# A list schedule with later K sets, a two-queue transfer model and second-stage sets not kept apart

## The chip, the cores and the metric

The kernel runs on one NeuronCore of a Trainium2 chip. The metric is the device time of one execution in microseconds (us). Five engines work side by side, each in its own instruction order: TensorE (PE; its weight loads are shown apart as PEld), VectorE (DVE), ScalarE (ACT), GpSimd (POOL) and SyncE (SP). Transfers between HBM and on-chip memory are issued from SP's, POOL's and ACT's queues. Matrix products land in PSUM banks, from which VectorE and ScalarE copy or combine them.

## The reference

Input `x` is 2048 tokens of 512 channels. A gate per token mixes two branches:

```python
g = sigmoid((x * gate_w).sum(-1, keepdims=True))
a = irfft(rfft(x^T, 2L) * rfft(K, 2L))[:L]^T + x * D_skip     # branch A, along the 2048 tokens
b = ((x @ w_gate) * (x @ w_up)) @ w_down                      # branch B, inner width 1792
out = g * a + (1 - g) * b
```

In branch A the convolution kernel is `K[d, l] = 2 Re(sum_n C[d,n] exp(A[d,n] dt[d] l))`, with 128 complex terms for each of the 512 channels; `A`, `C` and `dt` are computed from parameters.

## The kernel before

Branch B is most of the work. Each matmul operand in 32-bit precision is split in a high and a low part, and a product is three full-size matmuls (high x low, low x high, high x high), which the profile names by their tiles: `pg` and `pu` (gate and up products from tokens `xs` and weights `whi`, `wlo`), then `y` (down products from `hh`, `hl` and `dhi`, `dlo`). The 14 slices of the inner width are worked in four groups, and within a group the tokens in four blocks. VectorE multiplies `pu` by a copy of `pg` to `h`, ScalarE rounds `h` to `hh`, VectorE forms the rest `hl`. ScalarE scales finished `y` to `acc`, which is added to the output in HBM.

Branch A computes K and the transforms as small tiled matmuls between these. In 16 blocks of 32 channels, `phases`, `direct_powers`, `x_table` and `v_table` fill two tables, `x` and `v`, on VectorE and ScalarE; `k_block` multiplies them on TensorE, one K set of 128 matmuls into one bank (`k<-v,x`), and ScalarE and VectorE combine that to `kt`. After four blocks a quarter of the channels has its K. `k_first` transforms it (`k<-kt,w1k_t`, two sets) and stores it to `sk_d`; `u_part` has done the same with the input (`k<-in,w2s` in 64x512, eight sets early on) into `su_d`. `transforms` then runs, for each quarter, four second-stage sets (`m_second`, `k<-in,w2s` in 32x512; `x` or `v` in place of `in` in the last quarter), the products on VectorE (`m_product`), two inverse sets (`m_inverse`, `k<-y,w3s`) and the last stage (`m_last`, `k<-in,w4_t` or `k<-x,w4_t`, in the profile `w_t`). Data goes through HBM between the stages: POOL loads `su_d` and `sk_d`, SP stores and loads `y_d`.

All these small sets take their banks from one pool of four (`bank`, tag `k`). A K set takes one bank, the other sets take four at once, and a bank comes free when ScalarE or VectorE has read it.

The order of everything is a list schedule. Each piece of work is put down with `add(engine, us, fn, r=, w=, ...)`: its engine, a cost in the plan's time units and what it reads and writes. `Work.run` then repeatedly starts, of all pieces whose inputs are there, the one that can start first by the plan's own clock, with `rank` deciding between equals. Only the order that comes out of this is used: every engine issues its instructions in that order, and on the chip semaphores make them wait for one another. Three parts of the plan matter here:

- `inputs` and `ready`: a piece is ready when its inputs end in the plan, plus a small lag.
- `many`: a piece with `many > 0` starts no earlier than that many units behind the end of the last such piece on TensorE (`APART` = 6, `LESS` = 4 in the last two quarters). K sets, first-stage, second-stage and inverse sets of the K path have it.
- transfers: one bus in the plan, on which they run one after the other at `DMA_RATE`, with fixed lags.

All instructions are recorded through one helper, so nearly every row of the profile has its line, L124, and rows are told apart by their tiles.

Of the kernel before, what the change touches and what calls it, by code (L numbers as in the profile page):

```python
# [20 lines left out]
KT = D // P  # L21
# [94 lines left out]
class InOrder:  # L116


    def __init__(self, tc, engine):
        self.tc, self.engine, self.last = tc, engine, None  # L120
# [46 lines left out]
        self.deps, self.tiles, self.start, self.end, self.rows, self.many = set(), [], None, None, (), 0  # L167


class Work:  # L170


# [11 lines left out]


    APART, LESS = 6.0, 4.0
    DMA_RATE = 0.3

    def __init__(self):
        self.tags, self.tasks = {}, []  # L190
# [4 lines left out]
    def memory(self):  # L195
        return Tile(self, None, None, None, None, None, False)

    def add(self, engine, us, fn, r=(), w=(), rank=1, after=0.0, dma=0, hold=(), rows=(), many=0):


        task = Task(len(self.tasks), engine, us, fn, rank, after, dma)
        task.rows, task.many = rows, many
        self.tasks.append(task)
        clash = lambda p, q: p is None or q is None or p == q
        split = lambda x: x if isinstance(x, tuple) else (x, None)
        for tile, part in map(split, r):
            task.deps.update(t for p, t in tile.writers if clash(p, part))
        for tile, part in map(split, w):
            task.deps.update(t for p, t in tile.writers + tile.readers if clash(p, part))
        for tile, part in map(split, r):  # L210
            tile.readers.append((part, task))
        for tile, part in map(split, w):
            tile.writers.append((part, task))
        for tile, _ in map(split, [*r, *w, *hold]):
            if tile.pool and tile not in task.tiles:
                task.tiles.append(tile)
                tile.users.append(task)
        task.deps.discard(task)
        return task

    def ready(self, task, d):

        if d.engine == task.engine == "pe":
            return d.end
        return d.end + self.LAG.get(task.engine, 0.03) + (self.PE_LAG if d.engine == "pe" else 0.0)

    def inputs(self, task):

        at = task.after
        for d in task.deps:  # L230
            if d.end is None:
                return None
            at = max(at, self.ready(task, d))
        return at

    def slots(self, task, at):

# [30 lines left out]
    def run(self):  # L268
        left = {}
        for t in self.tasks:  # L270
            left.setdefault(t.engine, []).append(t)
        free = {e: 0.0 for e in left}
        bus, order, known, rows, apart = 0.0, [], {}, {}, -9.0
        while any(left.values()):
            best, wanted, found = None, {}, []
            for e, tasks in left.items():
                for t in tasks:
                    at = known.get(t)
                    if at is None:
                        at = self.inputs(t)  # L280
                        if at is None:
                            continue
                        known[t] = at
                    found.append((t, at))
                    if self.kept_waiting(t):
                        continue
                    for tile in t.tiles:
                        if tile.loose and tile.made is None:
                            wanted.setdefault(tile.key, []).append((t.rank, at))
            for t, ins in found:  # L290
                at = self.slots(t, ins)
                if at is None:
                    continue
                start = max([at, free[t.engine]] + [apart + t.many] * (t.many > 0) + [rows[r] for r in t.rows if r in rows])
                if any(
                    rank < t.rank and when <= start
                    for tile in t.tiles if tile.made is None and tile.loose for rank, when in wanted[tile.key]
                ):
                    continue
                key = (start, t.rank, t.n)  # L300
                if best is None or key < best[0]:
                    best = (key, t)
            assert best, "no work can start"
            (start, _, _), t = best
            left[t.engine].remove(t)
            if t.many:
                apart = start + t.us
            t.start, t.end = start, start + t.us
            free[t.engine] = t.end - self.OVERLAP.get(t.engine, 0.0)
            if t.dma:  # L310
                bus = max(bus, t.end + 1.3) + t.dma / self.DMA_RATE / 1000
                t.end = bus + 0.5
            rows.update((r, t.end) for r in t.rows)
            for tile in t.tiles:
                if tile.made is None:
                    tile.made = start
                    tile.had.append(tile)
            order.append(t)
        for t in order:
            t.fn()  # L320
        return order
# [3 lines left out]
def gated_mix_kernel(  # L325
# [19 lines left out]
    work = Work()  # L345
    add = work.add
# [247 lines left out]
    def evacuate(gi, ci, r, y):  # L594
        t = 4 * ci + r
        final = gi == len(GROUPS) - 1 and ci == LAST
        if final and r > 1:
            ending.append((r, y))
            return
        acc = new("glu", "acc", [P, D], bufs=3)  # L600
        add(
            "act", 0.69, lambda: act.activation(acc.t, y.t, AF.Copy, scale=ngate[:, t : t + 1]),
            r=[y, (m_gate, ci)], w=[acc], rank=0,
        )
        if final:
            ending.append((r, acc))
        elif gi == 0:
            add("sp", 0.42, lambda: sp.dma_start(ov[:, t, :], acc.t), r=[acc], w=[(m_out, t)], dma=256)
        else:
            add(  # L610
                "pool", 0.95, lambda: pool_q.dma_start(ov[:, t, :], acc.t, accum_op=ALU.add),
                r=[acc, (m_out, t)], dma=640, rows=[t],
            )

    def ends():
# [422 lines left out]
    def apart_of(q):  # L1038
        return work.LESS if q >= KT - 2 else work.APART

    def k_block(b, x, v):
        pk = bank()

        def kgen():
            pv = pk.t.rearrange("p (g j) -> p g j", j=64)
            for d in range(TB):
                ch, g = d % 4, d // 4
                for c in range(2):
                    pe.matmul(
                        pv[32 * ch : 32 * ch + 32, g, :], x.t[:, c, d, :], v.t[:, c, d, :], start=c == 0, stop=c == 1,  # L1050
                        tile_position=(0, 32 * ch),
                    )

        if b % 4 == 0:
            kts["now"] = new("tab", "kt", [P, 2, 2, 32, 16])
        kt, g0 = kts["now"], b % 4 * 8
        add("pe", 2.15, kgen, r=[x, v], w=[pk], rank=0, hold=[kt], many=work.APART)
        pv = lambda a: pk.t.rearrange("p (g a b k) -> p g a b k", a=2, b=2, k=16)[:, :, a]
        side = lambda h: kt.t[:, h, :, g0 : g0 + 8].rearrange("p b g k -> p g b k")
        add("act", 0.37, lambda: act.copy(side(1), pv(0)[:, :, :, ::-1]), r=[pk], w=[(kt, (1, b % 4))])  # L1060
        for h, op in enumerate((ALU.add, ALU.subtract)):
            add(
                "dve", 0.42, lambda h=h, op=op: dve.tensor_tensor(out=side(h), in0=pv(1), in1=side(1), op=op),
                r=[pk, (kt, (1, b % 4))], w=[(kt, (h, b % 4))], rank=0,
            )
        if b % 4 == 3:
            k_first(b // 4, kt)
# [89 lines left out]
    def m_second(q, T, ins, w):  # L1157
# [13 lines left out]
                to = banks[r].t[32 * c : 32 * c + 32].rearrange("l (p d) -> l p d", p=2)[:, p]  # L1171
                pe.matmul(to, w.t[lanes, m], src[lanes, c, p], start=True, stop=True, tile_position=(32 * r, 32 * c))

        add("pe", 1.05, fn, r=[*parts, w], w=banks, rank=1, hold=[to], many=apart_of(q))
        for r in range(4):
            h, e = divmod(r, 2)
            evict(
# [36 lines left out]
    def m_inverse(q, T0, ys, ws):  # L1214
# [18 lines left out]
                                    ys[t].t[lanes, k, e, cs], start=k == 0, stop=k == 1, tile_position=(32 * j, 64 * e),  # L1233
                                )

        add("pe", 2.13, fn, r=[*ys, *ws], w=[*banks, (m_turn, (q, T0))], rank=1, hold=sts, many=apart_of(q))
        for j in range(4):
            st, m = sts[j // 2], j % 2
            evict(
# [3 lines left out]
        for h in range(2):  # L1243
            st = sts[h]
            for p in range(2):
                b0 = 32 * (T0 + p) + 16 * h
                add(
                    "sp", 0.42,
                    lambda b0=b0, st=st, p=p: sp.dma_start(
                        y_d[q, b0 : b0 + 16].rearrange("(u e) n d -> (e n) u d", u=8),  # L1250
                        st.t[p::2].rearrange("p t i j d -> p (t i j) d"),
                    ),
                    r=[st], w=[(m_y, (q, T0 + h, p))], dma=256,
                )


# [7 lines left out]
    def m_last(q, gs):  # L1264
# [30 lines left out]
        for g, t, n0, n in pieces:  # L1295
# [30 lines left out]
            if n == 1 and n0 == LAST % 2:  # L1326
# [5 lines left out]
            add(  # L1332
                "pool", 0.95,
                lambda rs=rs, flat=flat: pool_q.dma_start(ov[:, rs[0] : rs[-1] + 1, cs], flat(), accum_op=ALU.add),
                r=[*parts, *((m_out, r) for r in rs)], dma=160 * len(rs), rows=rs,
            )

    def transforms(q):
# [111 lines left out]
```

## Time and profile before

| | |
|---|---|
| median of three runs | 591.4 us (590.39 to 591.89) |
| profiled execution | 592.45 us, of which the profile's span 590.6 us |
| TensorE busy | 576.8 us, 98% of the span |
| VectorE busy | 512.5 us, 87% |
| ScalarE busy | 400.0 us, 68% |
| GpSimd busy | 113.6 us, 19% |
| mean granted TensorE clock | 0.996 |

A row of a timeline reads: start, duration, engine, line, operation, the tiles written and read, shapes, count; in brackets the idle time ahead of it and what ended that. The granted clock (PEclk) is the share of full speed at which TensorE was allowed to run. Busy times of matmuls overlap, since they are pipelined: the cost of one in a row of equals is the step from start to start. The page's waits list who waited for whom: total, times, longest.

### The profile page before, as it was taken

How to read it: one execution, taken by the hardware profiler on the slowest of the kernel's cores; microseconds unless marked ns; L12 is line 12 of the kernel's file. 1: busy time of each engine (PE TensorE's matmuls, PEld its weight loads, DVE VectorE, ACT ScalarE, POOL GpSimd, SP SyncE). 2: the span in 40 equal slices, each digit the busy share in tenths (PEclk: the TensorE clock that was granted, in tenths of full speed). 3: DMA queues.
4: the chain of work that ended last, by engine and by line, in shares of the span. 5: the costliest groups of instructions: out<-in, count | busy, mean ns of one | idle time of the engine just before them, and what ended most of it. 6: DMA issues, size and time to landing. Idle time of an engine off the chain costs nothing.

```text
span 590.6 us, 14844 instructions
## 1 busy us (share of the span) xinstructions
PE 576.8 (98%) x5996; PEld 435.3 (74%) x5996; DVE 512.5 (87%) x812; ACT 400.0 (68%) x891; POOL 113.6 (19%) x159
## 2 busy tenths in 40 slices
PE   8899999998999999999999999999999999999996
PEld 5667777686786778788677877867777887677765
DVE  6997999999998999999999999996899992357745
ACT  5368787996679598968869775799596442433351
POOL 0011202331112141310122401113332103201011
PEclk9999999999999999999999999999999999999999
DMA  8998967699577697989739996999968539898886
GB/s 275 383 372 332 362 224 286 164 294 304 121 157 196 213 279 184 215 232 277 200 98 293 188 223 213 189 254 282 225 144 226 94 118 285 250 305 195 262 189 124
DMA packets 71687, 136.28 MB, mean 231 GB/s; under 512 B 6852, under 2 KB 35780, under 8 KB 69188
## 3 DMA queue, kind: packets, MB, share of 16 engines
q1 hardware_dynamic: 47668, 87.10, 43.5%
q0 software_dynamic: 23392, 47.98, 39.1%
q8 instruction: 47, 0.77, 0.5%
q10 hardware_dynamic: 560, 0.26, 0.2%
q14 instruction: 20, 0.16, 0.1%
HBM read 80.27 MB, written 55.05 MB: 229 GB/s over the span
## 4 chain that ended last, share of the span: by engine, by line
PE 85%; DVE 9%; ACT 2%; issue 2%; DMA 1%; DVEq 0%; SPq 0%; ACTq 0%
PE y L124 25%; PE pg L124 23%; PE pu L124 22%; PE k L124 16%; DVE v L124 2%; DVE x L124 2%; DVE hl L124 1%; DMA y<-in_xT 1%; DVE h L124 1%; DVE wlo L124 1%; DVE ri L124 1%; DVE m L124 1%; DVE t L124 0%; DVE y L124 0%; ACT ev L124 0%
## 5 line engine op out<-in xcount | busy, mean ns | idle before, releaser
L124 PE MATMUL pg<-xs,whi 128*128 128x512 f32 x448 | 138.7, 391 | 1.1 <-DVE xs L124 0.6
L124 PE MATMUL pu<-xs,whi 128*128 128x512 f32 x448 | 138.2, 390 | 0.0
L124 PEld LDWEIGHTS pg<-xs,whi 128*128 128x128 f32 x448 | 84.0, 188 | 20.6 <-ACT whi L124 2.0
L124 PEld LDWEIGHTS pu<-xs,whi 128*128 128x128 f32 x448 | 84.1, 188 | 17.0
L124 PE MATMUL y<-dhi,hl 128*128 128x512 f32 x224 | 90.6, 405 | 0.2
L124 PE MATMUL pg<-xs,wlo 128*128 128x512 f32 x224 | 89.4, 399 | 0.6 <-ACT whi L124 0.5
L124 PE MATMUL pu<-xs,wlo 128*128 128x512 f32 x224 | 89.6, 400 | 0.0
L124 PE MATMUL y<-dlo,hh 128*128 128x512 f32 x224 | 87.8, 392 | 1.4 <-DVE dlo L124 1.4
L124 PE MATMUL y<-dhi,hh 128*128 128x512 f32 x224 | 87.4, 390 | 1.5 <-issue 1.5
L124 POOL DMA_DIRECT2D out<-acc x44 | 39.1, 960 | 163.6 <-ACT acc L124 146.0
L124 ACT COPY ev<-k 128x512 f32<-128x512 f32 x112 | 59.2, 600 | 12.5 <-PE k L124 12.5
L124 ACT CAST hh<-h 128x512 fp32r<-128x512 f32 x56 | 34.6, 618 | 40.5 <-DVE h L124 40.2
L124 ACT ACTIVATE acc<-y,ngate 128x512 f32<-128x512 f32 x62 | 42.4, 692 | 25.4 <-PE y L124 24.5
L124 PEld LDWEIGHTS y<-dhi,hl 128*128 128x128 f32 x224 | 42.1, 188 | 23.6 <-issue 11.8
L124 ACT COPY h<-pg 128x512 f32<-128x512 f32 x56 | 33.1, 590 | 36.3 <-PE pg L124 29.1
L124 PEld LDWEIGHTS pg<-xs,wlo 128*128 128x128 f32 x224 | 42.0, 188 | 18.3 <-issue 7.4
L124 PEld LDWEIGHTS pu<-xs,wlo 128*128 128x128 f32 x224 | 42.0, 188 | 16.8 <-issue 7.9
L124 DVE TENSOR_TENSOR h<-pu,h 128x512 f32<-128x512 f32 x56 | 38.5, 688 | 14.0 <-PE pu L124 12.9
L124 PEld LDWEIGHTS y<-dhi,hh 128*128 128x128 f32 x224 | 42.2, 188 | 11.0 <-issue 1.9
L124 PEld LDWEIGHTS y<-dlo,hh 128*128 128x128 f32 x224 | 42.2, 189 | 9.6 <-DVE dlo L124 1.8
L124 DVE TENSOR_TENSOR hl<-h,hh 128x512 fp32r<-128x512 f32 x56 | 38.6, 689 | 4.7 <-ACT hh L124 4.6
L124 PEld LDWEIGHTS k<-v,x 128*32 128x32 f32 x2048 | 31.7, 111 | 8.8 <-issue 7.8
(130 smaller groups left out, 969.3 us busy)
## 6 DMA issues: line engine op xcount, KB each, us to landing
xs<-xs_d SPq DMA_DIRECT2D x36, 512.0 KB, 5.7
out<-acc POOLq DMA_DIRECT2D x44, 256.0 KB, 5.5
raw<-in_wts SPq DMA_DIRECT2D x33, 256.0 KB, 5.3
xs_d<-xs SPq DMA_DIRECT2D x16, 512.0 KB, 6.2
su_d<-ev POOLq DMA_DIRECT2D x32, 256.0 KB, 5.9
y_d<-ts SPq DMA_DIRECT2D x28, 256.0 KB, 5.7
in<-su_d POOLq DMA_DIRECT2D x12, 512.0 KB, 6.5
sk_d<-ev SPq DMA_DIRECT2D x6, 1024.0 KB, 6.3
```

The lines of the kernel that those rows point to most:

```text
L124: got = getattr(self.engine, name)(*args, **kw)
```

## The change

Five edits, all in the planner or in costs that it reads. No computation, tile or transfer is changed; only the order that the planner writes can differ.

- A piece can have a `slack`, which is added to the time at which its inputs are ready. K sets get 5 units (there are 16 blocks, so `b < 16` holds for all). The `slack` on `m_inverse` is zero in both branches.
- Second-stage sets (`m_second`) no longer have `many`: they are not kept apart from other sets, and others not from them.
- The plan's single bus becomes a class `Bus` with two queues, one for POOL's transfers and one for the others. While both have work, each gets half the rate, and the end of each transfer on the way is worked out anew whenever one is added. The rate goes from 0.3 to 0.33, and lags by engine (`SENT`, `LANDED`) replace the fixed ones.
- TensorE, ScalarE and VectorE pieces that read what a transfer brought are ready `SURE` = 2 units behind its end, past the plan's first 20 units.
- The sizes that the plan counts for three kinds of transfers change: adds to the output 640 to 554 and 160 to 203 a row, stores of `y_d` 256 to 335.

```diff
+class Bus:
+    def __init__(self):
+        self.now, self.queues = 0.0, ([], [])
+
+    def serve(self, queues, now, until):
+        done = []
+        while now < until and any(queues):
+            share = sum(map(bool, queues))
+            step = min([q[0][1] * share for q in queues if q] + [until - now])
+            now += step
+            for q in queues:
+                if q:
+                    q[0][1] -= step / share
+                    if q[0][1] < 1e-6:
+                        done.append((q.pop(0)[0], now))
+        return done
+
+    def add(self, task, at, us):
+        at = max(at, self.now)
+        self.serve(self.queues, self.now, at)
+        self.now = at
+        self.queues[task.engine == "pool"].append([task, us])
+        return self.serve([[[*x] for x in q] for q in self.queues], at, 1e9)
...
     APART, LESS = 6.0, 4.0
-    DMA_RATE = 0.3
+    DMA_RATE = 0.33
+
+    SENT = {"sp": 0.9, "act": 0.9, "pool": 1.4}
+    LANDED = {"sp": 1.0, "act": 1.0, "pool": 1.3}
+    SURE = 2.0
...
         if d.engine == task.engine == "pe":
             return d.end
+        if d.dma and d.start > 20.0 and task.engine in ("pe", "act", "dve"):
+            return d.end + self.SURE
...
-        return at
+        return at + task.slack
...
             if t.dma:
-                bus = max(bus, t.end + 1.3) + t.dma / self.DMA_RATE / 1000
-                t.end = bus + 0.5
+                for d, end in bus.add(t, t.end - 0.42 + self.SENT[t.engine], t.dma / self.DMA_RATE / 1000):
+                    d.end = end + self.LANDED[d.engine]
+                    for x in then.get(d, ()):
+                        known.pop(x, None)
...
-        add("pe", 2.15, kgen, r=[x, v], w=[pk], rank=0, hold=[kt], many=work.APART)
+        add("pe", 2.15, kgen, r=[x, v], w=[pk], rank=0, hold=[kt], many=work.APART, slack=5.0 if b < 16 else 0.0)
...
-        add("pe", 1.05, fn, r=[*parts, w], w=banks, rank=1, hold=[to], many=apart_of(q))
+        add("pe", 1.05, fn, r=[*parts, w], w=banks, rank=1, hold=[to])
```

More of the change, by code (lines that the diff above doesn't have):

```diff
@@ L196, in memory, with add @@
         return Tile(self, None, None, None, None, None, False)
-    def add(self, engine, us, fn, r=(), w=(), rank=1, after=0.0, dma=0, hold=(), rows=(), many=0):
+    def add(self, engine, us, fn, r=(), w=(), rank=1, after=0.0, dma=0, hold=(), rows=(), many=0, slack=0.0):
         task = Task(len(self.tasks), engine, us, fn, rank, after, dma)
-        task.rows, task.many = rows, many
+        task.rows, task.many, task.slack = rows, many, slack
         self.tasks.append(task)
@@ L272, in run @@
         free = {e: 0.0 for e in left}
-        bus, order, known, rows, apart = 0.0, [], {}, {}, -9.0
+        order, known, rows, apart = [], {}, {}, -9.0
+        bus, then = Bus(), {}
+        for t in self.tasks:
+            for d in t.deps:
+                if d.dma:
+                    then.setdefault(d, []).append(t)
         while any(left.values()):
@@ L611, in evacuate @@
                 "pool", 0.95, lambda: pool_q.dma_start(ov[:, t, :], acc.t, accum_op=ALU.add),
-                r=[acc, (m_out, t)], dma=640, rows=[t],
+                r=[acc, (m_out, t)], dma=554, rows=[t],
             )
@@ L1234, in fn @@
                                 )
-        add("pe", 2.13, fn, r=[*ys, *ws], w=[*banks, (m_turn, (q, T0))], rank=1, hold=sts, many=apart_of(q))
+        add("pe", 2.13, fn, r=[*ys, *ws], w=[*banks, (m_turn, (q, T0))], rank=1, hold=sts, many=apart_of(q), slack=0.0 if q < KT - 1 else 0.0)
         for j in range(4):
@@ L1252, in m_inverse @@
                     ),
-                    r=[st], w=[(m_y, (q, T0 + h, p))], dma=256,
+                    r=[st], w=[(m_y, (q, T0 + h, p))], dma=335,
                 )
@@ L1334, in m_last @@
                 lambda rs=rs, flat=flat: pool_q.dma_start(ov[:, rs[0] : rs[-1] + 1, cs], flat(), accum_op=ALU.add),
-                r=[*parts, *((m_out, r) for r in rs)], dma=160 * len(rs), rows=rs,
+                r=[*parts, *((m_out, r) for r in rs)], dma=203 * len(rs), rows=rs,
             )
```

## The prediction

> **What bounds the kernel now.** I read the page first (busy shares, then the chain that ended last), then TensorE's own waits, then the stretches around the largest of them.
>
> ```profile
> PE 576.8 (98%) x5996; PEld 435.3 (74%) x5996; DVE 512.5 (87%) x812; ACT 400.0 (68%) x891; POOL 113.6 (19%) x159
> ...
> PE 85%; DVE 9%; ACT 2%; issue 2%; DMA 1%; DVEq 0%; SPq 0%; ACTq 0%
> ```
>
> TensorE (PE) is busy 98% of the span and carries 85% of the chain. The change neither adds nor removes a matmul, so all it can move is TensorE's idle time, some 14 us, and what its clock loses by idling. Where that idle time lies:
>
> ```profile
> PE k L124 <- DVE v L124: 3.0, 1, 3.0
> ...
> PE y L124 <- issue: 1.5, 1, 1.5
> PE y L124 <- DVE dlo L124: 1.4, 1, 1.4
> ```
>
> The largest wait is one set of K matmuls (`k<-v,x`) that waits for the last VectorE (DVE) row of its table. The other two are single waits; "issue" names nothing that the profile sees, and I leave that one where it is. Here is the first, then a K set that waited for nothing:
>
> ```profile
> 139.81 0.39 PE L124 MATMUL y<-dhi,hl 128*128 128x512 f32 x1
> ...
> 140.94 0.39 PE L124 MATMUL y<-dhi,hh 128*128 128x512 f32 x1
> 144.28 3.12 PE L124 MATMUL k<-v,x 128*32 128x64 f32 x128 [2.95 <-DVE v L124]
> 147.33 0.80 PE L124 MATMUL y<-dhi,hl 128*128 128x512 f32 x1
> ...
> 148.63 0.39 PE L124 MATMUL y<-dhi,hl 128*128 128x512 f32 x1
> ...
> 165.45 2.07 PE L124 MATMUL k<-v,x 128*32 128x64 f32 x128
> 167.44 0.50 PE L124 MATMUL pu<-xs,wlo 128*128 128x512 f32 x1
> ...
> 168.24 0.40 PE L124 MATMUL pg<-xs,wlo 128*128 128x512 f32 x1
> ```
>
> A full-size matmul (128x512) costs 0.227 us: five steps from 139.81 to 140.94, though each row says 0.39, as neighbours overlap. The waiting set costs more than its 2.95 us. From its start to the next matmul it takes 3.05 us (147.33 - 144.28) where the other takes 1.99 (167.44 - 165.45), and the three matmuls behind it take 1.30 where the other's take 0.80. Together 2.95 + 1.06 + 0.50 = 4.5 us. The granted clock says why:
>
> ```profile
> 140.00:160.00 20.00, 17.00 (x186) 13.74 (x185) 18.79 (x29) 11.40 (x23) 2.32 (x3) 0.91 0.63 192
> 160.00:480.00 320.00, 318.55 (x3675) 243.77 (x3674) 302.67 (x448) 241.82 (x551) 67.48 (x74) 1.00 0.82 204
> ```
>
> The columns are stretch, length, busy PE, PEld, DVE, ACT, POOL, then the clock: 0.91 in the stretch with the wait, 1.00 in the 320 us behind it. [...]
>
> **The change part by part.** All parts act through the order that the planner writes.
>
> *K sets later behind their tables.* On TensorE, at the set that waits (third of the sixteen), before:
>
> ```order
> L124 MATMUL pu<-xs,whi 128x512 x2
> L124 MATMUL y<-dhi,hl 128x512
> L124 MATMUL y<-dlo,hh 128x512
> L124 MATMUL y<-dhi,hh 128x512
> L124 MATMUL y<-dhi,hl 128x512
> L124 MATMUL y<-dlo,hh 128x512
> L124 MATMUL y<-dhi,hh 128x512
> L124 MATMUL k<-v,x 32x64 x64
> L124 MATMUL y<-dhi,hl 128x512
> ```
>
> and in the changed order:
>
> ```order
> L124 MATMUL y<-dhi,hl 128x512
> L124 MATMUL y<-dlo,hh 128x512
> L124 MATMUL y<-dhi,hh 128x512
> L124 MATMUL k<-v,x 32x64 x64
> L124 MATMUL pg<-xs,wlo 128x512
> L124 MATMUL pg<-xs,whi 128x512 x2
> ```
>
> The set moved from the head of a run of down-projection matmuls (`y`) to its end. Counted from the program's start, 545 full-size matmuls stand ahead of it instead of 512, with the same ten smaller sets: 33 x 0.227 = 7.5 us later on TensorE. On VectorE two rows have come in ahead of the table's last row, one `su<-ri` and one `t<-pb,turns`:
>
> ```profile
> 143.52 0.62 DVE L124 TENSOR_TENSOR v<-v,sq 128x256 f32<-128x256 f32 x1
> 144.04 0.74 DVE L124 TENSOR_TENSOR su<-ri 128x576 f32<-128x576 f32 x1
> ...
> 145.68 0.84 DVE L124 TENSOR_TENSOR t<-pb,turns 128x672 f32<-128x672 f32 x1
> ```
>
> 0.74 + 0.84 = 1.6 us. The shortfall of 2.95 becomes a spare time of 7.5 - 1.6 - 2.95 = 2.9 us, so the wait goes: **-4.5**. Not less than -3.0 (only the idle part) and not more than -4.5.
>
> *The start.* The new transfer model also swaps VectorE rows in the first 25 us. Before (`x` is an exponential series for the tables, `y,gate` a row sum for the gate, `dlo` the low part of the down weights):
>
> ```order
> L124 SCALAR_TENSOR_TENSOR x<-x 128x512 x3
> L124 SCALAR_TENSOR_TENSOR y,gate<-in,w3s 128x512
> L124 SCALAR_TENSOR_TENSOR x<-x 128x512
> L124 SCALAR_TENSOR_TENSOR y,gate<-in,w3s 128x512
> L124 TENSOR_TENSOR dlo<-kt,dhi 128x512
> ```
>
> and in the changed order:
>
> ```order
> L124 SCALAR_TENSOR_TENSOR x<-x 128x512
> L124 SCALAR_TENSOR_TENSOR y,gate<-in,w3s 128x512
> L124 SCALAR_TENSOR_TENSOR x<-x 128x512
> L124 SCALAR_TENSOR_TENSOR y,gate<-in,w3s 128x512
> L124 TENSOR_TENSOR dlo<-kt,dhi 128x512
> ```
>
> Two `x` rows have gone behind `dlo`. TensorE waited for exactly that row:
>
> ```profile
> 20.41 2.14 DVE L124 SCALAR_TENSOR_TENSOR x<-x 128x512 f32<-128x512 f32 x3
> 22.46 0.68 DVE L124 SCALAR_TENSOR_TENSOR y<-in,w3s 128x512 f32<-128x512 f32 x1
> ...
> 25.03 0.50 PE L124 MATMUL y<-dlo,hh 128*128 128x512 f32 x1 [1.40 <-DVE dlo L124]
> ```
>
> Three `x` rows take 22.46 - 20.41 = 2.05 us, so two take 1.4, a little less where rows overlap, and the wait is 1.40: **-1.2** (ends 0, if the gate's input is late instead, and -1.4).
>
> *Second-stage sets no longer kept apart.* These sets (`k<-in,w2s`) write four PSUM banks of a pool of four, and the next set needs banks that ScalarE has emptied. On TensorE behind the sixth K set, before, ten rows go by with no other set; in the changed order:
>
> ```order
> L124 MATMUL k<-v,x 32x64 x64
> L124 MATMUL y<-dhi,hl 128x512
> L124 MATMUL y<-dlo,hh 128x512
> L124 MATMUL y<-dhi,hh 128x512
> L124 MATMUL pg<-xs,wlo 128x512
> L124 MATMUL pg<-xs,whi 128x512 x2
> L124 MATMUL pu<-xs,wlo 128x512
> L124 MATMUL pu<-xs,whi 128x512 x2
> L124 MATMUL k<-in,w2s 32x512 x16
> ```
>
> Nine full-size matmuls, 2.0 us, stand between two sets. Over the whole order, places where fewer than 16 (3.6 us) do: 4 before, 18 now. What such a place costs, the four before show; only one had a wait in it:
>
> ```profile
> 40.51 1.11 PE L124 MATMUL k<-in,w2s 32*64 32x512 f32 x16
> 41.55 0.50 PE L124 MATMUL pu<-xs,wlo 128*128 128x512 f32 x1
> ...
> 111.54 1.50 PE L124 MATMUL k<-in,w2s 32*64 32x512 f32 x16
> 112.97 0.50 PE L124 MATMUL y<-dhi,hl 128*128 128x512 f32 x1
> ```
>
> 1.43 us from start to next where the other took 1.04: 0.39 over. ScalarE was late with the banks, since other work stood between its copies:
>
> ```profile
> 109.38 1.05 ACT L124 COPY ev<-k 128x512 f32<-128x512 f32 x2
> 110.33 0.59 ACT L124 COPY h<-pg 128x512 f32<-128x512 f32 x1
> 110.80 1.09 ACT L124 COPY ev<-k 128x512 f32<-128x512 f32 x2
> ```
>
> So 0.39 in four places, 0.1 each. Fourteen more: **+1.4**, ends 0 and 14 x 0.39 = +5.5. I take the mean, as three of the four show nothing, the one with nine matmuls among them.
>
> *One more set.* The last stage's final two halves (`k<-x,w_t`) were one set of 32; now nine matmuls stand between them. A set of that shape:
>
> ```profile
> 560.29 0.61 PE L124 MATMUL pg<-xs,whi 128*128 128x512 f32 x2
> 560.84 1.95 PE L124 MATMUL k<-in,w_t 64*32 64x512 f32 x32
> 562.72 0.50 PE L124 MATMUL pg<-xs,wlo 128*128 128x512 f32 x1
> ```
>
> 1.88 us from start to next, and some 0.1 to enter it (0.32 from the second `pg` at 560.52 instead of 0.227). By the set of 16 above (1.04) two halves cost 2 x (1.04 + 0.1) = 2.3 against 2.0: **+0.3** (0 to 0.6). This set is also the tight place with nine matmuls ahead of it.
>
> *Transfers.* Loads, stores and adds change places on SP's and POOL's queues. TensorE waits on no transfer now. The tightest cover that I find is the last quarter's `x<-sk_d`:
>
> ```profile
> 514.02 1.86 POOL L124 DMA_DIRECT2D x<-sk_d  x2 [10.68 <-DMA sk_d<-e]
> ...
> x<-sk_d POOLq DMA_DIRECT2D x2, 512.0 KB, 6.4
> ...
> 526.01 1.14 PE L124 MATMUL k<-x,w2s 32*32 32x256 f32 x34
> ```
>
> Issued from 514.0, landed 6.4 us later at some 520.4, used at 526.0: 5.6 us of cover. From the first-stage sets (`k<-kt,w1k_t`) to this use, 54 full-size matmuls stand where 69 stood, 3.4 us less. 2.2 us of cover are left: **0** (up to +2 if that store and load each land a microsecond later).
>
> Sum: -4.5 - 1.2 + 1.4 + 0.3 = **-4.0**. The profiled execution took 592.45 us (span 590.6 and 1.85 around it), so 588.4 by it; it stands 1.05 above the median of the three runs, 591.4, so against those 591.4 - 4.0 = **587.4**.
>
> **The rivals.** *The wait moves to the next table.* TensorE would run 5.7 us earlier against a VectorE that is busy 302.67 of 320 us between 160 and 480. The next set started just behind its table:
>
> ```profile
> 164.36 0.63 DVE L124 TENSOR_TENSOR v<-v,sq 128x256 f32<-128x256 f32 x1
> ```
>
> It ends at 164.99, the set starts at 165.45: 0.46 spare. In the new order 27 more matmuls stand ahead of that set (+6.1) and one more 0.69 us row on VectorE; less the 5.7, some 0.2 us are spare. Further on VectorE's 17.3 us of idle time must shrink for the rest of the gain to last. For this speaks that K sets are not all that wait on VectorE: the `hl` rows have had no added distance. Against it, that idle time, and that all later sets get more matmuls ahead or fewer VectorE rows. Where VectorE yields nothing, all 5.7 come back, and the 1.7 of bank waits and the extra set lie inside those waits: 591.4, no change.
>
> *Slower: banks.* The place is the fourteen new neighbours. ScalarE works 75% of the time between 160 and 480 (241.82 of 320), in order, in rows of 0.6 to 1.1 us. If a set finds ScalarE behind by one 0.59 us copy each time, 14 x 0.59 = 8.3 in place of 1.4: 587.4 + 6.9 = 594.3. It turns slower than before by 0.3% from (4.0 + 1.4 + 1.8) / 14 = 0.51 us a place. The row at 111.54 (0.39, with a 0.59 us copy between) says it can come near that; the three places without a wait speak against it. *The same with the clock.* If each such pause dropped the clock, as the 2.95 us one did at 1.5 us, the price would be near 2 us a place, over 610. No short pause of this trace did that: 1.00 from 160 to 480. [...]
>
> *Faster still.* The "issue" wait of 1.45 us does not recur: 586.
>
> **How the numbers follow.** Results within 0.3% (1.8 us) of 591.4 are about what a measurement here can't tell from no change. Forecast (584.5 to 589.5): 0.50; faster still, some below it: 0.08; the wait moves (589.6 to 593.2): 0.20; banks: 0.18; banks with the clock, or a late transfer: 0.04. Faster 0.58, same 0.20, slower 0.22. Low end: all costs at zero and the "issue" wait gone, 591.4 - 4.5 - 1.4 - 1.5 = 584.0. High end: the banks' case, 594.5. Above it lies the clock case, below it little.
>
> **What would show it.** Right: the profile after has no K set with a wait over 0.5 us, the clock at 1.00 between 140 and 160, the wait on `dlo` under 0.4, and new TensorE waits for ScalarE or for banks below 3 us in all. Wrong: a wait of a K set or of `y<-dhi,hl` on VectorE of 2 us or more, with a stretch of lower clock behind it; or many second-stage sets over 1.3 us long; or a TensorE wait on `x<-sk_d`.

## The result and the profile after

| | before | changed |
|---|---|---|
| median | 591.07 us (589.91 to 591.89, 6 runs) | 588.17 us (586.28 to 589.07, 6 runs) |
| profiled execution, its span | 592.45, 590.6 us | 588.43, 586.6 us |
| mean granted clock | 0.996 | 1.00 |

The ratio is 0.9949, with an interval of 0.993 to 0.9968: 0.5% or 3.0 us faster. The forecast of 587.4 was 0.8 us low, and of the 4.0 us forecast 3.0 came. As will be seen, its sum came out nearly right because its errors cancel.

The changed kernel's page, busy shares and chain:

```profile
PE 576.4 (98%) x5996; PEld 433.9 (74%) x5996; DVE 511.3 (87%) x812; ACT 399.0 (68%) x891; POOL 113.4 (19%) x159
...
PE 83%; DVE 6%; ACT 4%; DMA 4%; issue 1%; SPq 0%; DVEq 0%; ACTq 0%
```

All work has its old length within 0.4% (TensorE busy 576.4 us against 576.8, VectorE 511.3 against 512.5), and only the places of the idle time differ. TensorE's own waits in the changed kernel, the whole list (us in total, times, longest):

```profile
PE y L124 <- DVE hl L124: 2.4, 2, 1.6
PE k L124 <- DVE acc L124: 1.5, 1, 1.5
PE k L124 <- issue: 0.6, 1, 0.6
PE pg L124 <- DVE xs L124: 0.6, 1, 0.6
PE pg L124 <- ACT whi L124: 0.5, 1, 0.5
PE pg L124 <- ACT h L124: 0.4, 1, 0.4
PE y L124 <- ACT acc L124: 0.2, 1, 0.2
```

The K set's 3.0 on `v` and the 1.4 on `dlo` are gone. No wait is for a bank of the small sets (`ev`, `kt`). New at the top are two waits of down products for VectorE's `hl`. The stretches that were shown of before, with the clock as the last column but two:

```profile
140.00:160.00 20.00, 19.26 (x204) 15.58 (x203) 19.62 (x30) 11.43 (x22) 3.41 (x4) 1.00 0.78 198
160.00:480.00 320.00, 318.37 (x3671) 243.14 (x3670) 302.64 (x450) 241.01 (x551) 64.77 (x70) 1.00 0.79 202
```

The clock stays at 1.00 where it was 0.91, and TensorE works 19.26 us of the 20 instead of 17.00.

The two new waits on TensorE's timeline:

```profile
141.22 0.39 PE L124 MATMUL y<-dhi,hh 128*128 128x512 f32 x1
142.35 0.50 PE L124 MATMUL y<-dhi,hl 128*128 128x512 f32 x1 [0.74 <-DVE hl L124]
...
171.66 0.61 PE L124 MATMUL pg<-xs,whi 128*128 128x512 f32 x2
173.91 0.50 PE L124 MATMUL y<-dhi,hl 128*128 128x512 f32 x1 [1.63 <-DVE hl L124]
```

And VectorE ahead of the second:

```profile
169.13 2.09 DVE L124 TENSOR_TENSOR x<-m,x 128x896 f32<-128x896 f32 x2
171.14 0.42 DVE L124 TENSOR_TENSOR kt<-k,kt 128x256 f32<-128x256 f32 x1
171.47 0.68 DVE L124 TENSOR_TENSOR h<-pu,h 128x512 f32<-128x512 f32 x1
172.07 0.42 DVE L124 TENSOR_TENSOR kt<-k,kt 128x256 f32<-128x256 f32 x1
172.40 0.85 DVE L124 SCALAR_TENSOR_TENSOR t<-rt,t 128x672 f32<-128x672 f32 x1
173.16 0.69 DVE L124 TENSOR_TENSOR hl<-h,hh 128x512 fp32r<-128x512 f32 x1
```

VectorE has no gap. `h` stands behind two table rows (`x<-m,x`), `hl` behind one more (`t<-rt,t`), and TensorE waits for `hl`, which needs `h`. The table work that no longer holds up the K set holds up the down products instead.

The end differs too. The start of the last matmul and the last transfer, before, with that transfer's row of the list of transfers (the last number is us from issue to landing):

```profile
585.52 0.39 PE L124 MATMUL y<-dhi,hh 128*128 128x512 f32 x1
...
586.86 0.35 ACTq L124 DMA_DIRECT2D out<-kt  x1
...
out<-kt ACTq DMA_DIRECT2D x1, 128.0 KB, 2.8
```

and in the changed kernel:

```profile
582.46 0.39 PE L124 MATMUL y<-dhi,hh 128*128 128x512 f32 x1
...
583.79 0.35 ACTq L124 DMA_DIRECT2D out<-kt  x1
...
out<-kt ACTq DMA_DIRECT2D x1, 128.0 KB, 1.7
```

Both issue it 1.33 us behind the last matmul's start. It lands 1.0 us sooner in the changed kernel, where the last half set stands 48 full-size matmuls from the end and GpSimd's last addition to the output is long issued (the last two of before, then the last of the changed kernel):

```profile
579.01 2.86 POOL L124 DMA_DIRECT2D out<-x  x2 [8.51 <-DVE x L124]
```

```profile
575.02 1.28 POOL L124 DMA_DIRECT2D out<-x  x1 [0.79 <-DVE kt L124]
```

To compare whole runs I take from each trace how much longer than usual the steps of TensorE were: from start to start, over 0.227 us for a full-size matmul, and over the usual length of each kind of set. Summed by stretch (us), with "end" for the time from the start of the last matmul to the end of the span:

| run | to 11 us | 11 to 40 | 40 to 200 | from 200 | end | span |
|---|---|---|---|---|---|---|
| before | 0.2 | 3.2 | 5.8 | 2.3 | 5.1 | 590.6 |
| changed | 0.6 | 1.1 | 4.0 | 2.4 | 4.1 | 586.6 |
| third K set later by hand | 2.0 | 2.6 | 4.5 | 2.2 | 4.9 | 590.5 |
| third and fourth later | 0.7 | 3.9 | 6.2 | 1.0 | 5.0 | 591.2 |
| two `x` rows behind `dlo` | 0.5 | 2.5 | 5.6 | 1.4 | 4.9 | 588.7 |
| distance alone | 2.4 | 2.6 | 5.6 | 0.7 | 7.4 | 593.5 |
| transfer model alone | 2.0 | 1.1 | 4.6 | 6.6 | 10.2 | 599.2 |
| sets not apart alone | 0.2 | 3.2 | 6.7 | 2.5 | 4.2 | 591.0 |
| distance, sets not apart | 1.1 | 2.6 | 4.4 | 1.7 | 5.7 | 590.0 |
| changed, without distance | 2.4 | 1.2 | 5.8 | 1.3 | 4.1 | 589.3 |
| changed, sets apart | 2.4 | 1.1 | 4.0 | 1.7 | 4.1 | 588.6 |
| changed, `hl` earlier | 0.2 | 1.4 | 3.3 | 1.3 | 4.1 | 584.9 |
| changed, and four more rows | 0.9 | 1.1 | 2.7 | 1.4 | 4.1 | 585.0 |
| changed, last set late | 0.2 | 1.3 | 4.2 | 1.4 | 8.6 | 590.4 |

What is left in each row, the matmuls themselves, is 574 to 575 us. The first column is slow matmuls while the program starts (steps of 0.43 us). It differs between executions of one order (the changed kernel and the one with sets apart have the same rows on TensorE there, 0.6 and 2.4), so spans of single profiles carry some 2 us of chance; the ratios below come from many runs. The profiled execution of the transfer model alone took 601.1 us against its median of 596.0, so its 6.6 is above what is typical.

### The profile page after: what moved, and what is told of

Read it like the earlier page. It is cut to its first block, busy times and chain, and to the rows that moved or that the text cites. A ratio compares the mean times of both kernels' runs of the same rounds, so it can differ in the third digit from the quotient of the medians.

```text
span 586.6 us, 14827 instructions
## 1 busy us (share of the span) xinstructions
PE 576.4 (98%) x5996; PEld 433.9 (74%) x5996; DVE 511.3 (87%) x812; ACT 399.0 (68%) x891; POOL 113.4 (19%) x159
## 4 chain that ended last, share of the span: by engine, by line
PE 83%; DVE 6%; ACT 4%; DMA 4%; issue 1%; SPq 0%; DVEq 0%; ACTq 0%
PE pg L124 23%; PE pu L124 23%; PE y L124 22%; PE k L124 16%; DVE v L124 1%; DMA pb<-par_d 1%; DMA xs_d<-xs 1%; DVE x L124 1%; DMA y<-in_xT 1%; DMA xs<-xs_d 1%; ACT acc L124 1%; DVE t L124 1%; ACT ev L124 1%; ACT xs L124 1%; ACT e L124 1%
```

## Experiments

The theories: **A**, a K set that stands late enough gives back its 4.5 us for good, and the terms add up. **B**, in the first 200 us VectorE and ScalarE set the pace, so that TensorE, let past one row, waits at the next; and what the change gains lies elsewhere.

### One K set later, by hand

In the kernel before, the third K set is put behind 15 more full-size matmuls in the finished list. The other engines' rows stay.

```diff
+EDIT = ((2, 5),)
...
+        for n, ahead in EDIT:
+            k = [t for t in order if "kgen" in t.fn.__qualname__][n]
...
+            pes = [t for t in order[at + 1 :] if t.engine == "pe"][:ahead]
...
+            order[at:at] = [*pes, k]
```

(Third K set, five pieces of three matmuls each.)

> The kernel before, with one thing moved on TensorE: the third K set stands 15 full-size matmuls (3.4 us) later; all other engines keep their order. Theory A (the wait was a lone one and its price, 2.95 us idle and 1.5 us of slow clock, is saved for good): 4.5 us less, 0.992 of before. Theory B (VectorE sets the pace from table to table): TensorE reaches the fourth K set 4.5 us earlier, its table ends at most 0.7 us earlier and had 0.46 us to spare, so the fourth set waits 3 to 3.5 us and the clock falls there; in all within 1.5 us of before, 0.997 to 1.000.

590.49 us, ratio 0.9991 (0.9971 to 1.0011): nothing gained. The K set waits no more. The first of TensorE's waits, and its timeline 10 us further on:

```profile
PE y L124 <- ACT acc L124: 1.8, 1, 1.8
...
155.99 0.61 PE L124 MATMUL pu<-xs,whi 128*128 128x512 f32 x2
158.46 0.50 PE L124 MATMUL y<-dhi,hl 128*128 128x512 f32 x1 [1.85 <-ACT acc L124]
...
159.95 0.59 PE L124 MATMUL y<-dhi,hl 128*128 128x512 f32 x1
160.33 0.63 PE L124 MATMUL y<-dlo,hh 128*128 128x512 f32 x1
...
163.32 0.44 PE L124 MATMUL y<-dhi,hh 128*128 128x512 f32 x1
```

A down product now waits 1.85 us for a bank that ScalarE's `acc` has to read, and some 1.5 us behind it eight matmuls run at 0.43 us instead of 0.227 (159.95 to 163.32), another 1.6. The wait went to another row with its slow clock (0.83 from 156 to 166 us). Theory B's number came, but not the wait that it named: the fourth K set, where it expected 3 to 3.5 us, waits for nothing.

### Two K sets later

The same with the fourth K set as well.

```diff
-EDIT = ((2, 5),)
+EDIT = ((2, 5), (3, 5))
```

> As the run with the third K set 15 matmuls later, and the fourth K set 15 matmuls later as well. Theory A: nothing more than the one set gave, 0.992. Theory B: the wait at the fourth set goes as well, and as the fifth had 4.3 us to spare the gain now stays: 0.992 here, where the run with one set showed little of it.

592.97 us, ratio 1.0013 (0.9999 to 1.0028). Both theories had 0.992 here, so neither number came. What fits B is that waits move on: they are now for `acc` (1.9), `h` on VectorE (1.8) and `h` on ScalarE (1.3), and the stretch from 40 to 200 loses 6.2 us, more than before.

### The start alone

The kernel before, with two of the `x` rows of VectorE (`series`) put behind `dlo` rows (`rests`), as the change does it.

```diff
+        early = [t for t in series if t in dve[:gates]]
+        slots = [None if t in early[-3:-1] else t for t in order]
...
+            if t is not None and t in rests[1:3]:
+                seq.append("slot")
```

> The kernel before, with two rows of the exponential series (x) on VectorE put behind the three dlo rows in the first 35 us; the other engines keep their order. Both theories: the wait on dlo at 23 us falls from 1.4 us to under 0.3. Theory A: 1.2 to 1.4 us less, 0.998. Theory B: TensorE only arrives earlier at the third K set, whose wait grows from 2.95 to some 4.2 us, and the time is that of before, 1.000.

590.89 us, ratio 0.9978 (0.9963 to 0.9992): 1.3 us gained. TensorE's start, and its largest wait (the row counts the 97 of the set's 128 matmuls that start before 146 us, where this view ends):

```profile
23.11 0.39 PE L124 MATMUL y<-dhi,hl 128*128 128x512 f32 x1
23.48 0.50 PE L124 MATMUL y<-dlo,hh 128*128 128x512 f32 x1
...
143.44 2.85 PE L124 MATMUL k<-v,x 128*32 128x64 f32 x97 [2.94 <-DVE v L124]
```

The `dlo` wait is down to 0.14. The K set starts 0.84 us earlier than before (144.28), in spite of slow matmuls at the start, and its wait did not grow from 2.95: the rows behind came earlier too. Theory A holds for this term; B had 4.2 us for that wait and no gain.

### The parts of the change, alone and in pairs

Distance is the `slack` of 5 on K sets, transfers the two-queue model with its rates, lags and sizes, and not apart the second-stage sets without `many`. Each kernel has the named parts and is otherwise the kernel before.

| parts | median us | ratio to before |
|---|---|---|
| distance | 593.39 | 1.0033 (1.0011 to 1.0055) |
| transfers | 596.03 | 1.0088 (1.0051 to 1.0126) |
| not apart | 591.15 | 0.9984 (0.9964 to 1.0004) |
| distance, not apart | 592.38 | 1.0013 (0.9992 to 1.0034) |
| transfers, not apart | 592.64 | 1.0001 (0.9980 to 1.0022) |
| transfers, distance | 588.17 | 0.9943 (0.9923 to 0.9963) |
| all three | 588.17 | 0.9949 (0.9930 to 0.9968) |

*Without the distance:*

```diff
-        add("pe", 2.15, kgen, r=[x, v], w=[pk], rank=0, hold=[kt], many=work.APART, slack=5.0 if b < 16 else 0.0)
+        add("pe", 2.15, kgen, r=[x, v], w=[pk], rank=0, hold=[kt], many=work.APART, slack=0.0)
```

> The changed kernel with the five time units of the K sets taken out again; the transfer model and the second-stage sets stay as changed. Its order puts the third K set 1 full-size matmul later than before (518 ahead of it where the changed order has 545, counted from its sets; before 512), with 20 tight places between sets. Theory A (the distance is what removes the wait, 4.5 us of it, and the rest of the change is worth the 1.7 us of the start): a K set waits for VectorE's table row again, 2 to 3 us in one place, and the time is about 4 us above the changed kernel's, ratio to before 0.997 to 1.000. Theory B (VectorE and ScalarE set the pace in the first 180 us, so that a wait taken from a K set comes back at a down-projection matmul): the waits of TensorE for VectorE between 130 and 180 us, which were 2.4 us at `y<-dhi,hl` in the changed kernel, stay 2 to 3.5 us in all and only change place, and the ratio stays 0.994 to 0.996.

3 us slower than the changed kernel, nearly as A has it (ratio 1.0001, where it had 0.997 to 1.000), but with B's picture: K sets wait only 0.9 us for a table, and the rest of the 5.8 us from 40 to 200 lies at `pg`, `y` and other sets. The distance is worth 1.9 us there (5.8 against 4.0 in the table, before rounding). Where the rest of the 3 us lies is not shown: the profiled execution took 591.2 us, 1.5 less than the median, and 1.8 us of its span's 2.7 over the changed kernel are slow matmuls at the start.

*Second-stage sets kept apart again:*

```diff
-        add("pe", 1.05, fn, r=[*parts, w], w=banks, rank=1, hold=[to])
+        add("pe", 1.05, fn, r=[*parts, w], w=banks, rank=1, hold=[to], many=apart_of(q))
```

> The changed kernel with the second-stage sets kept apart as before: 6 tight places instead of 18, the first five K sets where the change puts them. My forecast's term (0.1 us at a tight place, 0.39 where a bank is late): 12 places fewer, 1.2 us less than the changed kernel, ratio to before about 0.993. The rival (a tight place costs nothing): the same as the changed kernel, 0.995. If keeping the sets apart was what cost time elsewhere (K sets or the last sets pushed back): above 0.996. In each case the waits at `y<-dhi,hl` near 141 and 172 us stay, as the order there is the same.

The same ratio as the changed kernel, with 6 tight places for 18, as the rival had it. The ratio alone does not decide it, as the forecast's 0.993 lies within the interval. The groups of second-stage sets say more, busy us and mean ns, before and then in the changed kernel:

```profile
L124 PE MATMUL k<-in,w2s 32*32 32x512 f32 x378 | 13.7, 600 | 0.0
L124 PE MATMUL k<-v,w2s 32*32 32x512 f32 x64 | 2.3, 600 | 0.0
```

```profile
L124 PE MATMUL k<-in,w2s 32*32 32x512 f32 x378 | 14.6, 600 | 0.0
...
329.48 2.09 PE L124 MATMUL k<-in,w2s 32*32 32x512 f32 x32
...
330.51 0.14 PEld L124 LDWEIGHTS k<-in,w2s 32*32 32x32 f32 x5 [0.82 <-issue]
```

All of the 0.9 us is in one set, at 329.48, whose last five weight loads came 0.82 us late for "issue"; the others kept their length. That set is itself a tight place, 15 matmuls behind a K set, but it did not wait for a bank: the last row that read one (`kt<-k,kt` on VectorE) ended at 327.73, 1.75 us ahead of it.

*The distance alone:*

```diff
-        add("pe", 2.15, kgen, r=[x, v], w=[pk], rank=0, hold=[kt], many=work.APART)
+        add("pe", 2.15, kgen, r=[x, v], w=[pk], rank=0, hold=[kt], many=work.APART, slack=5.0)
```

> The kernel before with the five time units for the K sets alone: third K set behind 542 full-size matmuls instead of 512, second-stage sets apart, rows of the start as before. Theory A (the distance removes the wait for good): no K set waits more than 0.5 us for VectorE, the wait at the start for `dlo` stays 1.4, and the time is 3 to 4.5 us below before, ratio 0.9925 to 0.995. Theory B (the wait moves, as when the one set was moved by hand with the other engines left alone): 1.5 to 2.5 us of new waits for `hl`, `acc` or `h` between 140 and 180 us, 0.997 to 1.000.

Slower than before, outside both theories' numbers. B's part is there: no K set waits 0.5 us for a table, but 0.7 us for a transfer and 1.9 for `acc` stand at 146 to 150 us, with the clock at 0.83 behind them (148 to 158 us). Of 5.8 us from 40 to 200, 0.2 are gained. What neither theory had is the end, 7.4 us for 5.1. The end of its chain:

```profile
577.14 1.59 PE y L124 x6
581.99 2.02 DVE x L124 x5
584.01 2.05 DVE kt L124 x6
```

The last half set stands 21 matmuls from the end, and the rows of VectorE that follow from it outlast TensorE.

*The transfer model alone:*

```diff
+class Bus:
...
-    DMA_RATE = 0.3
+    DMA_RATE = 0.33
+
+    SENT = {"sp": 0.9, "act": 0.9, "pool": 1.4}
+    LANDED = {"sp": 1.0, "act": 1.0, "pool": 1.3}
+    SURE = 2.0
```

> The transfer model alone (two queues, new rates and sizes, two units behind a transfer), without distance for the K sets and with second-stage sets apart. By the terms of the sum: the start's gain of 1.2 to 1.7 us is there, the K wait of 2.95 is there or takes another size of 2 to 4 us, ratio 0.997 to 0.999. The rival: the new model alone spreads the work so that the K set no longer waits, and the distance adds nothing: 0.994 to 0.996.

Neither number came. The start's gain is there (1.1 for 3.2 from 11 to 40), and the K set's wait is down from 2.95 to 0.3 us without any distance, as the rival had it; the time did not follow. The last half set stands 9 matmuls from the end, whose chain ends like the one above but 10.2 us behind the last matmul: 5 us more than before, as much as the median lost.

*Sets not apart alone:* the same edit as in the changed kernel, for itself.

> The kernel before with the second-stage sets not kept apart, and nothing else: 19 tight places instead of 4, the first five K sets and the rows of the start where they were. By my forecast's term, 0.1 us for each of 15 more places and 0.3 for one more set: 1.8 us slower, ratio about 1.003. If a tight place costs nothing, as with the sets put apart again in the changed kernel: the K wait of 2.95 us and the `dlo` wait of 1.4 stay, one more set costs 0.3, and the transfer after the last matmul may land up to 1 us sooner: ratio 0.998 to 1.001.

19 tight places, and no wait for a bank; the term's 1.003 lies outside the interval (0.9964 to 1.0004). The wait of the K set is 2.8, `dlo` 1.4, and the end 4.2 instead of 5.1, with the last half set again 48 from the end. What this part gains in its trace lies at the end rather than where it acts; the ratio is not clear of 1. One tight set, at 322.40 us, stood still for "issue" and took 1.7 us longer:

```profile
PE k L124 <- issue: 1.2, 1, 1.2
```

Here too the last read of a bank had ended (at 322.04). But in the seven kernels that keep second-stage sets apart, none of these sets (`32*32`) took over 0.2 us more than usual, and in five of the seven that do not, one did, by 0.8 to 1.7 us, always at a tight place (four of the five share nearly one order). Whether tight places bring such stalls is not shown: the kernels that keep the sets apart have them at other rows, as before at 416 us (1.45).

*Distance and sets not apart:* both edits, with the transfer model of before.

> The kernel before with the distance of the K sets and the second-stage sets not kept apart, the transfer model left as before: the last pairing of the three parts. Its last half set stands 27 full-size matmuls from the end (21 with the distance alone, 48 in the changed kernel), and the `dlo` wait of the start is there. Theory B (the end and the waits that have moved decide, not the number of waits of K sets): between the runs with 21 and with 48, some 6 to 6.5 us behind the last matmul, the start's 1.5 us not gained, 4 to 6 us of waits between 40 and 200 us: ratio 0.999 to 1.003. Theory A (the distance brings its 4.5 us wherever the rest allows it, and the loss with the distance alone came from keeping sets apart): 0.992 to 0.996.

Theory B's number. No K set waits for a table, and `acc` takes over:

```profile
PE y L124 <- ACT acc L124: 2.7, 2, 2.5
...
PE y L124 <- DVE dlo L124: 1.3, 1, 1.3
```

### The last set late

The changed kernel with the last half set moved back from 48 to 12 matmuls ahead of the end, to measure the end by itself.

```diff
             hold=[to for _, to, _, _ in pieces],
+            slack=8.0 if q == KT - 1 and gs == (LAST // 2,) else 0.0,
```

> The changed kernel with the last half of the last stage's set 12 full-size matmuls from the end instead of 48; on TensorE nothing else moves. If the rows of VectorE behind that set make the end (as the chain of work says of the two runs whose last set stood 21 and 9 from the end and whose spans went on for 7.4 and 10.3 us behind the start of the last matmul, where the changed kernel's goes on for 4.1): about 9.5 us behind the last matmul, span and time 5 to 6 us above the changed kernel's, ratio to before 1.003 to 1.006. If those two ends were long for another reason (late transfers of other rows): 0.994 to 0.996, as the changed kernel.

592.47 us, ratio 1.0015 (0.9994 to 1.0036), 0.66% above the changed kernel's ratio, or 3.9 us. The end of the chain:

```profile
578.17 1.10 PE k L124 x16
579.70 2.02 DVE x L124 x5
581.72 2.92 DVE kt L124 x7
```

The span goes on for 8.6 us behind the last matmul's start (9.5 expected). The time grew by less than the 5 to 6 us expected. That the last set's place can make the end is thereby shown: nothing else was moved on TensorE, and on VectorE and ScalarE only two rows each changed places behind it.

### Rows of VectorE and ScalarE earlier

The changed kernel with `h`, `hh` and `hl` ahead of table rows: at 172 us `h` right behind what it reads, then one table row, then `hl`; at 141 us `hl` ahead of one table row.

```diff
+        behind(h, last)
+        behind(x, h)
+        behind(hh, x)
+        behind(hl, hh)
...
+        behind(hh, h)
+        behind(hl, v)
```

> The changed kernel, with the rows that TensorE waits for at 141 us (0.74) and 172 us (1.63) put ahead of two to four table rows on VectorE, and their roundings ahead of one row each on ScalarE; TensorE keeps its order. If those waits are on the path: 1.5 to 1.9 us less than the changed kernel, 0.992 of before. If VectorE as a whole sets the pace, the table rows put behind make a later row late, and the time stays at 0.995 of before.

587.27 us, ratio 0.9918 (0.9898 to 0.9937): faster than before, and than the changed kernel by 1.8 us by the ratios, 0.9 by the medians. Of the two places' 2.7 us, 1.7 are gained, 0.85 comes back as a wait for `acc` at 177 us. In the next run four rows of ScalarE were put earlier as well, that `acc` among them:

```diff
+        for late_row, ahead in ((60, 57), (75, 73), (138, 136), (197, 195)):
+            row = acts[late_row]
+            behind(row, max([*row.deps, acts[ahead]], key=order.index))
```

> The changed kernel with the `h`, `hh` and `hl` rows of the earlier run moved ahead, and four rows of ScalarE besides: `acc` ahead of two `ev` copies at 56 us, `h` ahead of `rt` at 67, `acc` ahead of `v` and `sq` at 116, `acc` ahead of the sine `t` at 174. If each of these waits of TensorE is the matter of one row's place (0.48, 0.60, 0.36 and 0.85 us over the usual in the run before this): about 1.2 to 1.8 us less than that run, ratio to before 0.988 to 0.990. If VectorE and ScalarE set the pace there, so that the waits only move on: the same as that run, 0.991 to 0.993.

586.83 us, ratio 0.9923 (0.9893 to 0.9952): the same as the run before. Three of the four waits are gone, that at 68 us stayed, and the `hl` wait at 141 us is back. TensorE's row there, with `hl` earlier and then with the four rows besides:

```profile
142.00 0.50 PE L124 MATMUL y<-dhi,hl 128*128 128x512 f32 x1 [0.26 <-DVE hl L124]
```

```profile
142.60 0.50 PE L124 MATMUL y<-dhi,hl 128*128 128x512 f32 x1 [1.13 <-DVE hl L124]
```

VectorE's rows there stand in the same order in both, with hardly a gap. `hl` ends 0.6 us later, and TensorE, freed of a wait of 0.36 us at 117, is there 0.27 us earlier (141.74 and 141.47 without the wait). One reason for the later `hl` is likely but was not tried by itself: at 116 us `acc` went ahead of ScalarE's `v` and `sq`, for which VectorE's table rows wait. That VectorE bounds the gain, as theory B has it, fits these rows but is not shown by itself: 0.990, the least gain of theory A, lies just within the interval.

## Why the forecast was right, and where its steps failed

- **K sets, -4.5.** The wait and the slow clock went, as forecast: the set that cost 4.6 us over the usual (4.1 with its wait and 0.6 behind it) costs nothing. The time didn't follow. From 40 to 200 us the loss fell from 5.8 to 4.0, by 1.8 only, since the two `hl` waits took 2.7 us from start to start. The step that failed is the one from "the shortfall becomes a spare time of 2.9" to "so the wait goes: -4.5": it looked at the set that was moved, and not at who waits next for the same engine. The rival that the wait moves had the right mechanism, with `hl` named in it, but was priced as all or nothing; it happened by more than half. The four runs that move K sets in the order of before (by hand, or by the distance) show it more sharply: none is clearly faster than before. Nor does the wait hang on the distance alone: with the transfer model and no distance it was 0.3 us, and 0.9 with the sets not apart as well. The signs named for "right" nearly all came, the clock of 1.00 and the missing waits among them, but they ask whether the wait is gone and not who waits next.
- **The start, -1.2.** Right. Alone it measured 1.3 us. In the changed kernel the stretch from 11 to 40 us fell by 2.1 in the trace, of which `dlo` is 1.6.
- **Tight places, +1.4.** Mis-sized: as bank waits 0. The mean of one wait in four places was no price of a tight place. The 0.39 at 111.54 came from one `h` copy between the `ev` copies there, and it is there again in the run with sets not apart alone (0.42), while the other places had none. What a tight place did lose, 0.95 us at 329 us, was for "issue", which the term did not have.
- **One more set, +0.3.** Right: the two halves cost 0.26 over one set.
- **The end.** Not in the sum at all. The changed order's last half set stands six matmuls earlier, and the last transfer lands 1.0 us sooner: -1.0. That the six matmuls are the reason is not shown: without the distance the last half stands 39 from the end, nearer than the 42 of before, and the transfer lands in 1.7 us all the same. What goes with the landing is how long before the start of the last matmul GpSimd's last addition has been issued: 1.9 us (distance, sets not apart; it lands in 3.4), 3.7 (before; 2.8), 5.0 (without distance; 1.7), 6.2 (changed; 1.7). No run changes that alone. In three of the runs above this term was far larger (+2.3, +4.5 and +5.1 us against before or the changed kernel), enough to use up the whole gain.
- **Transfers 0, "issue" unchanged.** No wait for `x<-sk_d` appeared. The "issue" wait at 416 us didn't recur, but sets that took 0.95 us longer at 329 and 0.97 at 490 came in its place.

By stretches the spans' 4.0 are 1.7 at the start, 1.8 from 40 to 200 us and 1.0 at the end, less 0.2 from 200 us and 0.3 in the sets' own lengths. The forecast counted 2.7 us too much at the K sets; against that stand 1.4 of cost at the tight places that did not come as such, and 0.5 at the start and 1.0 at the end that it did not count. That the result lay 0.8 from it is partly luck.

What stays open: why the transfer model needs the distance (1.0088 to 0.9943). The traces put 6 us of it at the end and the rest at waits whose places differ in every order; which edge of the plan moves the last set to 9 matmuls from the end was not tried.

## To carry to other kernels

When two engines are nearly as busy as the one that sets the time (VectorE 95% and ScalarE 81% of the stretch from 40 to 200 us before), price the removal of a wait by what the next rows of the late engine allow, not by the length of the wait: of 4.6 us here 1.8 remained. In a list schedule each rule rewrites the order to the end, so look in the new order for who is last there and how much work stands behind it. Put parts together before judging them: here two parts that lose time alone (0.3% and 0.9%) gain 0.6% as a pair.

## What was not expected of the hardware

- In one run the clock fell behind a wait shorter than the 2.95 us of before, and in another it did not fall behind the same wait. The hand-moved orders wait in the same place for the same row, 2.0 us from start to start over the usual. In the stretch around it the one with one set moved ran at 0.83, the one with two at 1.00:

```profile
156.00:166.00 10.00, 8.15 (x45) 6.06 (x45) 9.97 (x16) 8.79 (x19) 2.57 (x3) 0.83 0.77 112
```

```profile
156.00:166.00 10.00, 8.14 (x36) 6.41 (x35) 9.96 (x15) 8.78 (x17) 2.57 (x3) 1.00 0.78 114
```

  Behind other waits the clock was 0.83 (1.9 us, distance alone, 148 to 158 us), 0.91 (2.8 us, sets not apart alone, 140 to 160 us, as with the 2.95 of before) and 1.00 (2.5 us, distance and sets not apart, 140 to 160 us). In the run with one set moved the slow stretch was 3.4 us (159.95 to 163.32) and cost 1.6. The length of a wait alone thus did not decide it; what did is not shown.
- At the start, matmuls at 0.43 us lasted until 6.7 us in one execution (changed) and until 10.8 in another whose rows on TensorE are the same there (changed, sets apart), with 1.00 as the clock shown for both: 1.8 us between executions that no row on TensorE explains.
- A set of 32 small matmuls stood still in its middle for "issue" in four runs: the one at 329 us took 0.8 to 0.95 us more in the changed kernel and in the three others with nearly its order (`hl` earlier, four more rows, last set late). It thus belongs to the order; its cause was not found.
